# The second mixture of experts as a straight line of tiles, with small tiles between the steps of full ones

## The chip, the cores and the metric

One NeuronCore of a Trainium2 chip runs the whole program. The metric is device time in microseconds of one execution. The kernel before took 1133.65 us, the median of three runs (1132.84 to 1135.4).

## What is computed

Three layers follow one another: an attention with pooled queries, a dense two-layer block (the first mixture), and the second mixture of experts, the only part that the change touches. Its reference, cut to what matters:

```python
def _moe2_ref(x, w_skip, w_gate, w1, w2):          # x 2304 x 512, 8 experts, 512 -> 1024 -> 512
    do_compute = x @ w_skip > 0
    out = x.copy()
    xc = x[do_compute]
    logits = xc @ w_gate
    e_idx = np.argmax(logits, axis=1)
    ...
    for e in range(E):
        mask = e_idx == e
        if not mask.any():
            continue
        h = np.maximum(xc[mask] @ w1[e], 0.0)
        y[mask] = gate_w[mask, None] * (h @ w2[e])
    out[do_compute] = xc + y
```

How many rows an expert gets is known only while the kernel runs.

## The kernel before

Attention and the dense block fill the first 950 us or so. While they run, `Router` places every row in a list in device memory, by expert, and counts. `Router.order` (L525 to L540) sorts the experts by their number of rows. From there on the program speaks of slots k = 0 to 7, the largest expert first. `o[:,0]` holds a slot's number of tiles of 128 rows, `o[:,1]` whether its last tile has at most 32 rows, `o[:,4]` the expert's number.

`Experts.run` (L694 to L778) is the second mixture. Two tiles, "a" and "b", of the expert that is largest so far are begun before the last rows are counted; the slots hold the rest. One full tile is:

- `gather` (L624): an indirect DMA, issued by GpSimd (POOL), brings 128 rows of x into SBUF;
- `turn` (L626): four PE transposes, and a copy out of PSUM on ScalarE (ACT) or VectorE (DVE);
- `layer1` (L635): the product with w1 into two PSUM tiles `ph`, with a relu on ACT (`hh`) and its remainder on DVE (`hl`);
- `layer2` (L650): 24 matmuls of 512 columns with w2 split into a high part `w2hi` and a low part `w2lo`, then `res` on DVE and `put` (L648), an indirect DMA on POOL that scatters the rows into the output.

`split` (L617) makes w2hi on ACT and w2lo on DVE, once for each expert that has full tiles. `few` (L663) handles a tile of at most 32 rows without the split: the product `ph`, a relu `hs`, two transposes, a copy `hT`, the product `py`, four small `res` and a `put`. Its steps wait for each other (PE, ACT, PE, ACT, PE, DVE), and `few` puts the `turn` of two later tiles between them.

`load` (L612) fetches the 4 MB of one expert's w1 and w2 in four DMAs from SyncE's queue (SP). There are three places for weights, a ring W[k%3]; `behind` (L609) lets a POOL memset take the waits for a place's memory.

What sets the order of the work is a tree of branches (L722 to L778). Every engine loads the counts into registers (`values`, L541), and for each slot it asks: is there a load for slot k+2 (L738, SP), has the slot rows (L739), has its last tile at most 32 (L746), is there another tile j (L755 with L757; L755 is the line that the profile names), more than the table ST has (L768), are there gathers for the next slot (L732, POOL). Each engine runs its own copy of the branches. An engine's instructions are issued in the order in which they are written.

```python
for k in range(E):
    if k+2<E:
        with tc.If(ns[k+2]>0): s.load(k+2,ee[k+2])
    with tc.If(n[k]>0) as some:
        with tc.If(few[k]>0) as one:
            s.few(k,xf(k),s.lf[k][:,0],gf(k),f"{k}e",turns(nc.vector))
        with one.Else():
            ...
        with ExitStack() as st:
            for j in range(s.ST[k]):
                st.enter_context(tc.If(n[k]>j+1))
```

With the inputs that are timed, PE executes in this order the tiles a, b, 0f and 0_0 (slot 0), 1e, 1_0 and 1_1 (slot 1), 2f (slot 2), 3e, 4e and 5e (slots 3 to 5); a name with e is a `few` tile, the others are full. Slots 6 and 7 have no rows.

Of the kernel before, what the change touches and what calls it, by code (L numbers as in the profile page):

```python
# [397 lines left out]
class Router:  # L398

    def __init__(s,tc,cp,ident,w9,w9t,NT,E,dram):  # L400
# [7 lines left out]
        s.r7=cp.tile([1,E],F32,name="r7");  # L408
# [4 lines left out]
    def setup(s):  # L413
# [9 lines left out]
        G.tensor_scalar(out=s.far,in0=s.pid,scalar1=float(2*P*s.COLS),scalar2=None,op0=ALU.add)  # L423
        G.memset(s.onesb,1.0)
# [139 lines left out]
    def rest(s,psL):  # L564
# [8 lines left out]
        V.tensor_tensor(out=o[:,3],in0=o[:,3],in1=o[:,2],op=ALU.add)  # L573
        s.o=o
        return [s.values(o[:,i],m) for i,m in ((2,(E-1)*s.TPE+2),(3,E*s.TPE-1),(4,E-1))]

class Experts:

    def __init__(s,tc,router,w1,w2,x2d,out,xT,cp,hp,rp):
        nc=tc.nc; s.tc,s.nc,s.r,s.out,s.x2d,s.hp,s.rp=tc,nc,router,out,x2d,hp,rp  # L580

        s.ST=(4,4,3,3,2,2,2,1)
# [7 lines left out]
    def alloc(s,ctx,psT,psL):  # L590
        tc,E=s.tc,s.r.E
        s.xp=ctx.enter_context(tc.tile_pool(name="exp",bufs=2))
        for k in ("f0","f1","n0","n1"): s.xt[k]=s.xp.tile([P,4,P],F32,name="xt"+k,bufs=1)
# [3 lines left out]
        for k in [f"f{k}" for k in range(E)]+["g0","g1","m0","m1","n0"]: s.xg[k]=one.tile([P,512],F32,name="xg"+k)  # L597
        s.lt=[one.tile([P,s.r.TPE,3],I32,name=f"lt{k}") for k in range(E)]
        s.lf=[one.tile([P,1,3],I32,name=f"lf{k}") for k in range(E)]
# [7 lines left out]
        s.xg["n1"]=s.xg["a"]  # L607
        s.own={"f0":(psL,"lg"),"f1":(s.psY,"py"),"e":(psT,"xt")}
    def behind(s,k):  # L609

        s.nc.gpsimd.memset(s.W[k%3][0][0][:1,0,:1],0.0)
    def load(s,k,e):  # L612
        for t,v in zip(s.W[k%3],(s.w1v,s.w2v)):
            for h in range(2):
                src=v[ds(e,1)][0]
                s.nc.sync.dma_start(t[h],src[:,:,h*512:h*512+512] if v is s.w1v else src[:,4*h:4*h+4])
    def split(s,k,part=("hi","lo"),hs=(0,1),e=None):  # L617

        nc=s.nc
        for h in hs:  # L620
            r,hi,lo=s.W[k%3][1][h],s.hi[h],s.lo[h]
# [10 lines left out]
    def psum1(s,own,nm):  # L632
        p,t=s.own.get(own,(s.psH,"ph"))
        return p.tile([P,4,P],F32,tag=t,name="ph"+nm)
    def layer1(s,k,x,nm,hs,own=None):  # L635
        nc=s.nc; w1=s.W[k%3][0]
        hh=s.hp.tile([P,2,4,P],F32R,tag="xh",name="hh"+nm); hl=s.hp.tile([P,2,4,P],F32R,tag="xl",name="hl"+nm)
        for h in range(2):
            ph=s.psum1(f"{own}{h}",f"{nm}_{h}")
# [10 lines left out]
    def layer2(s,k,lt,g,nm,hs,j=0,own=None):  # L650
# [9 lines left out]
        res=s.res[2 if own else j%2]  # L660
        nc.vector.scalar_tensor_tensor(out=res,in0=py,scalar=lt[:,1:2].bitcast(F32),in1=s.xg[g],op0=ALU.mult,op1=ALU.add)
        s.put(res,lt)
    def few(s,k,x,lt,g,nm,between):  # L663

        nc=s.nc; n=s.r.FEW; w1,w2=s.W[k%3]; cols=lambda j: slice(j*n,(j+1)*n)
        both=s.psum1("e",nm).rearrange("p f c -> p (f c)"); ph,ht=both[:,:256],both[:,256:].rearrange("p (f c) -> p f c",f=2)
# [8 lines left out]
        for _ in between: pass  # L675
# [18 lines left out]
    def run(s,steps,psL):  # L694
# [3 lines left out]
        with ExitStack() as c:  # L698
# [20 lines left out]
            for k in range(2,E): lists(k)  # L719
# [137 lines left out]
```

## Time and profile before

| what | us |
|---|---|
| median of three runs | 1133.65 |
| the profiled execution, its own time | 1134.37 |
| its span, first to last instruction | 1132.6 |
| PE busy (share of the span) | 1060.0 (94%) |
| DVE, ACT, POOL busy | 749.6, 590.0, 347.4 |

The profile was taken of one execution. Its time of 1134.37 us is the span and 1.77 us around it; it lies 0.72 us above the median. The profile names engines PE (TensorE), PEld (its weight loads), DVE, ACT, POOL and SP; a letter q behind a name is that engine's sequencer, where branches, register loads and semaphores run, which do not count as busy. PEclk is the granted TensorE clock as a share of 2.4 GHz; 0.50 is 1.2 GHz. A bracket behind a row of the timeline is the idle time just before it and what ended that.

### The profile page before, as it was taken

The page shows a single profiled execution, that of the slowest core. Times are in us where ns is not written, and L with a number is a line of the kernel's source. Part 1 is how long each engine was busy: PE and PEld are TensorE (multiplying, and loading weights), DVE is VectorE, ACT ScalarE, POOL GpSimd, SP SyncE. Part 2 cuts the span into 40 slices and gives each one's busy share as a digit, 9 for nine tenths or more (in the row PEclk, how much of TensorE's full clock was granted, in tenths as well). Part 3 has the DMA queues.
Part 4 walks back from the last instruction along what each step waited for, and adds up shares of the span by engine and source line. Part 5 has one row for each costly group of instructions (what it writes and reads, how often), then busy time and mean ns, then how long its engine had stood idle before and what let it go on. Part 6 is the DMA issues. An engine that isn't in the chain of part 4 may idle for free. (4 is left out here: it accounts for less than half of the span.)

```text
span 1132.6 us, 20661 instructions
## 1 busy us (share of the span) xinstructions
PE 1060.0 (94%) x7463; PEld 862.6 (76%) x7463; DVE 749.6 (66%) x1870; ACT 590.0 (52%) x1366; POOL 347.4 (31%) x505
## 2 busy tenths in 40 slices
PE   7999999999999999999889999999999999998952
PEld 6677777777677777776679999999999988887831
DVE  6788777887788777875777467777776754313220
ACT  5788778887788787875443333333233324112200
POOL 4466554555666544540430000000000002241000
PEclk8999999999999999999999999999999999998986
DMA  8776646656775556521541101101011015584440
GB/s 215 173 182 183 171 131 160 170 161 172 181 181 168 141 156 154 152 70 47 164 129 64 38 20 38 38 2 38 1 38 39 1 39 205 177 275 166 171 162 8
DMA packets 67661, 135.25 MB, mean 119 GB/s; under 512 B 10684, under 2 KB 19900, under 8 KB 67520
## 3 DMA queue, kind: packets, MB, share of 16 engines
q1 hardware_dynamic: 65056, 127.64, 39.4%
q0 software_dynamic: 2464, 5.80, 1.8%
q8 instruction: 80, 1.31, 0.5%
q14 instruction: 61, 0.50, 0.1%
HBM read 94.63 MB, written 20.17 MB: 101 GB/s over the span
## 5 line engine op out<-in xcount | busy, mean ns | idle before, releaser
L163 PE MATMUL t<-ident,p 128*128 128x128 f32 x1152 | 197.8, 281 | 8.4 <-ACT PT L168 7.8
L163 PEld LDWEIGHTS t<-ident,p 128*128 128x128 f32 x1152 | 137.7, 141 | 70.4 <-ACT PT L168 27.4
L168 ACT ACTIVATE PT<-t 128x384 f32<-128x384 f32 x288 | 140.3, 492 | 61.5 <-PE t L163 57.6
L348 PE MATMUL ph<-xh,wih 128*128 128x256 f32 x576 | 162.3, 282 | 9.4 <-DVE e L354 8.5
L178 PE MATMUL o<-PT,v 128*64 128x256 f32 (+1 forms) x1152 | 170.3, 418 | 0.0
L348 PE MATMUL ph<-xh,wil 128*128 128x256 f32 x576 | 160.7, 279 | 0.2 <-DVE wil L329 0.2
L348 PE MATMUL ph<-xl,wih 128*128 128x256 f32 x576 | 160.6, 279 | 0.0
L113 PE MATMUL s<-ks,qh 128*128 128x384 f32 x384 | 131.6, 397 | 4.6 <-ACT qh L65 2.6
L120 DVE TENSOR_REDUCE m<-s 128x1 f32<-128x768 f32 x128 | 122.4, 956 | 16.4 <-PE s L113 5.2
L356 ACT ACTIVATE gh<-e 128x256 fp32r<-128x256 f32 x144 | 60.3, 419 | 139.2 <-DVE e L354 139.2
L83 POOL TENSOR_TENSOR kl<-kr,kh 64x288 fp32r<-64x288 f32 x120 | 97.0, 839 | 94.8 <-ACT kh L79 87.8
L348 PEld LDWEIGHTS ph<-xh,wih 128*128 128x128 f32 x576 | 108.1, 188 | 21.0 <-issue 14.2
L352 ACT ACTIVATE e<-ph 128x256 f32<-128x256 f32 x144 | 54.9, 382 | 126.3 <-PE ph L348 125.9
L522 POOL DMA_INDIRECT rowlist<-meta,sl x18 | 18.3, 1019 | 333.2 <-DVE sl L521 330.4
L136 ACT ACTIVATE p<-s,nb 128x768 f32<-128x768 f32 x128 | 115.2, 900 | 0.0
L366 PE MATMUL px<-woh,gh 128*128 128x512 f32 x288 | 114.6, 398 | 0.0
L366 PE MATMUL px<-wol,gh 128*128 128x512 f32 x288 | 113.7, 395 | 0.0
L353 DVE TENSOR_SCALAR e<-e 128x256 f32<-128x256 f32 x144 | 56.4, 392 | 86.4 <-ACT e L352 85.1
L348 PEld LDWEIGHTS ph<-xl,wih 128*128 128x128 f32 x576 | 108.4, 188 | 5.0
L366 PE MATMUL px<-woh,gl 128*128 128x512 f32 x288 | 112.1, 389 | 0.0
L167 DVE COPY PT<-t 128x384 f32<-128x384 f32 x144 | 79.5, 552 | 48.9 <-PE t L163 47.5
L113 PE MATMUL s<-ks,ql 128*128 128x384 f32 x384 | 111.2, 344 | 0.0
(304 smaller groups left out, 2021.1 us busy)
## 6 DMA issues: line engine op xcount, KB each, us to landing
qr<-qT SPq DMA_DIRECT2D x64, 288.0 KB, 8.5
w<-w SPq DMA_DIRECT2D x16, 1024.0 KB, 11.6
v<-vt SPq DMA_DIRECT2D x32, 288.0 KB, 3.1
kr<-kT SPq DMA_DIRECT2D x15, 576.0 KB, 6.2
ks<-kh SPq DMA_DIRECT2D x30, 288.0 KB, 4.0
ks<-kl SPq DMA_DIRECT2D x30, 288.0 KB, 3.3
d<-w_in SPq DMA_DIRECT2D x16, 512.0 KB, 8.9
d<-w_out SPq DMA_DIRECT2D x16, 512.0 KB, 3.8
```

The costliest lines, as they stand in the source:

```text
L83: for c in range(0,S,S//4): e.tensor_tensor(out=st["kl"][o,c:c+S//4],in0=st["kr"][r,c:c+S//4],in1=st["kh"][r,c:c+S//4].bitcast(F32),op=ALU ...
L113: nc.tensor.matmul(dst[:,ci,:S3],st[n][j][:,t*P:t*P+P],st["ks"][j][:,c*S3:c*S3+S3],start=first,stop=last)
L120: nc.vector.tensor_reduce(out=m2[:,0:1],in_=s2[:,:,:S3],op=ALU.max,axis=AX.XY)
L136: nc.scalar.activation(pt[:,:2*S3].rearrange("p (c s) -> p c s",c=2),d["s2"][:,:,:S3],AF.Exp,bias=d["nb"],scale=SC,accum_out=a2[:,n,0:1])
L163: nc.tensor.transpose(po[:,c],pt[:,(g*3+c)*P:(g*3+c+1)*P],ident)
L167: if evac[g]: nc.vector.tensor_copy(o,s)
L168: else: nc.scalar.activation(o,s,AF.Copy)
L178: nc.tensor.matmul(cell["o"][64*a:64*a+64,:n],state[pr]["v"][a][:,c],src[:,c,a,:n],start=(c==0),stop=(c==NC-1))
L348: nc.tensor.matmul(ph[:,:TB],w[:,cc],x[:,cc],start=(n==0),stop=(n==3*KC-1)); n+=1
L353: nc.vector.tensor_scalar(out=e,in0=e,scalar1=1.0,scalar2=-1.0,op0=ALU.min,op1=ALU.add)
L356: nc.scalar.activation(gh,e,AF.Copy)
L366: nc.tensor.matmul(X[b][t][:,:DM],a[:,t*P:(t+1)*P],w,start=(f==0 and i==0),stop=(f==KF-1 and i==2))
```

## The change

Two tables of constants take the place of the tree. `TILES=(2,2,1,0,0,0,0,0)` says how many full tiles each slot gets and `SMALL=(0,1,0,1,1,1,0,0)` whether it gets a small one. The tiles are written as one line of code, and the small ones are cut into their steps (`few` is now a generator): few(3) runs between the steps of tile (1,0), and few(1,2) and few(4) alternate. What the tables don't cover is counted into `s.more`; behind one branch at the end there are loops over the remaining tiles for all eight slots.

```diff
+        s.TILES=(2,2,1,0,0,0,0,0); s.SMALL=(0,1,0,1,1,1,0,0)
...
+        for e in range(E): G.memset(s.tiles[:,e:e+1],float(s.TILES[e])); G.memset(s.small[:,e:e+1],float(s.SMALL[e]))
...
-        V.tensor_tensor(out=o[:,3],in0=o[:,3],in1=o[:,2],op=ALU.add)
+        V.tensor_tensor(out=fw,in0=o[:,1],in1=s.small,op=ALU.mult)
+        V.tensor_tensor(out=o[:,1],in0=o[:,0],in1=fw,op=ALU.subtract)
+        V.tensor_tensor(out=o[:,1],in0=o[:,1],in1=s.tiles,op=ALU.subtract)
+        V.tensor_scalar(out=o[:,1],in0=o[:,1],scalar1=0.0,scalar2=None,op0=ALU.max)
+        with s.nc.allow_low_precision(reason="whole numbers"): V.tensor_reduce(out=s.more,in_=o[:,1],op=ALU.add,axis=AX.X)
...
-        s.ST=(4,4,3,3,2,2,2,1)
+        s.ring=(0,1,2,2,0,1,0,0); s.TILES,s.SMALL=router.TILES,router.SMALL
...
-        hs=s.hp.tile([P,2,4,P],F32R,tag="xh",name="hs"+nm).bitcast(F32).rearrange("p a b c -> p a (b c)")[:,0,:256]
+        hs=s.xp.tile([P,256],F32,tag="fs",name="hs"+nm)
         nc.scalar.activation(hs,ph,AF.Relu)
-        next(between)
+        yield
...
-            lists(0); lists(1)
-            first(0); more(0,0); first(1)
+            for k in (0,1,3): lists(k)
+            for k,j in ((0,0),(0,1),(3,0),(1,0)): bring(k,j)
             for _ in l1: pass
             s.split(0,"lo",(1,))
-            s.behind(1); s.load(1,ee[1])
-            for k in range(2,E): lists(k)
+            s.behind(1)
+            for k in (2,4,5): lists(k)
+            s.load(1,ee[1]); s.load(3,ee[3])
+            for k,j in ((1,1),(1,2),(4,0),(2,0),(5,0)): bring(k,j)
...
+            tile(0,0,last=lambda: turn(0,1))
+            tile(0,1,last=lambda: (turn(3,0),turn(1,0,nc.vector)))
+            s.load(4,ee[4])
+            s.split(1)
+            few(3,0,0)
+            tile(1,0,{1:[go(3)],6:[go(3)]},lambda: turn(1,1))
+            s.load(2,ee[2])
+            tile(1,1,last=lambda: (turn(1,2),turn(4,0,nc.vector)))
+            s.split(2)
+            few(1,2,1)
+            few(4,0,0)
+            turn(2,0); turn(5,0,nc.vector)
+            go(1)(); go(4)(); go(1)()
+            s.load(5,ee[5])
+            go(4)()
+            tile(2,0)
+            few(5,0,1)
+            go(5)(); go(5)()
+
+            with tc.If(r.values(r.more,E*r.TPE,None)[0]>0):
+                n=r.values(r.o[:,0],r.TPE,None); left=r.values(r.o[:,1],r.TPE,None)
+                for k in range(E):
+                    with tc.If(left[k]>0):
+                        s.ringd=s.ring; s.ring=(0,)*E
+                        s.load(k,ee[k])
+                        s.split(k)
+                        with tc.For_i(s.TILES[k],n[k],1) as j:
...
```

In the new code `tile(k,j,during,last)` is layer1, then `last()`, then layer2; `during` maps a step of layer1 (eight steps, 0 to 7) to what runs behind it, and `go(k)` runs the next step of few(k). The table `ring` says which of the three places of weights a slot uses.

Two places of the new order are shown, on PE and on SP. First PE, from the end of slot 3 to the end of tile 4e in the kernel before (`ph4e`, `py4e`: the two products of the small tile; `pt`: a turn):

```order
L755 UNCONDITIONAL_BRANCH x3
L739 UNCONDITIONAL_BRANCH
L738 UNCONDITIONAL_BRANCH
L739 COMPARE_AND_BRANCH
L732 UNCONDITIONAL_BRANCH x2
L746 COMPARE_AND_BRANCH
L668 MATMUL ph4e<-w_1_0_11918,xtf_11877 32x256 x2
L629 MATMUL pt5f<-ident,xgf_11893 128x128 x4
L672 MATMUL ph4e<-ident,hs4e 128x128 x2
L629 MATMUL pt_0_14573<-ident,xgg_11896 128x128 x4
L678 MATMUL py4e<-w_1_0_11920,hT4e 32x128 x16
L746 UNCONDITIONAL_BRANCH
```

Three tests (L739, L732 on POOL only, L746) and the jumps to them stand ahead of the tile, and one jump behind it.

The same tile on PE in the changed kernel, with its neighbours (`pf` is the small tile's first product; the row before is the end of tile (1,1), the last one the start of tile (2,0)):

```order
L664 MATMUL py_1_12620<-w2lo_11905,hh_1_12568 128x512 x4
L675 MATMUL pf1e<-w_1_0_11924,xt_11896 32x256 x2
L675 MATMUL pf4e<-xT,xt_11897 32x256 x16
L637 MATMUL pt_0_12691<-ident,xg_11919 128x128 x4
L637 MATMUL pt_0_12697<-ident,xg_11922 128x128 x4
L679 MATMUL pf1e<-ident,hs1e 128x128 x2
L679 MATMUL pf4e<-ident,hs4e 128x128 x2
L685 MATMUL py1e<-w_1_0_11926,hT1e 32x128 x16
L685 MATMUL py4e<-xT,hT4e 32x128 x32
L647 MATMUL ph_0_0_12797<-xt_11898,w_2_0_11928 128x128 x16
```

No branch stands between the tiles any more, and the first step of the second small tile and two turns stand where the first one waits for ACT. (Rows that repeat a step with another half of the weights are left out.)

Second SP's queue, in the kernel before, around the loads of slots 2 and 3:

```order
L738 COMPARE_AND_BRANCH
L616 DMA w_2_1_11925<-w 128x4x512
L738 UNCONDITIONAL_BRANCH x2
L739 COMPARE_AND_BRANCH
L746 COMPARE_AND_BRANCH
L755 COMPARE_AND_BRANCH x2
L732 UNCONDITIONAL_BRANCH
L768 COMPARE_AND_BRANCH
L738 COMPARE_AND_BRANCH
L616 DMA xT<-w 128x4x512
```

SP walks through the same tests as the computing engines before it comes to the next slot's load.

And in the changed kernel, the last list and the first and last piece of some loads (w_1 is place 1, w_2 place 2, xT place 0):

```order
L715 DMA lt_11911<-rowlist 128x9
L624 DMA w_1_0_11924<-w 128x4x512
L624 DMA w_1_1_11927<-w 128x4x512
L624 DMA w_2_0_11928<-w 128x4x512
L624 DMA xT<-w 128x4x512
L624 DMA w_2_1_11931<-w 128x4x512
L624 DMA w_1_0_11924<-w 128x4x512
L546 TENSOR_LOAD more
L768 COMPARE_AND_BRANCH
```

All lists now come ahead of the first load; the loads of slots 1 and 3 follow each other at once, then those of slots 4, 2 and 5, each held only by the readers of its place.

## Rows read from the trace of the kernel before

**Rows 1.** The page's first line: the span.

```profile
span 1132.6 us, 20661 instructions
```

**Rows 2.** Windows: busy us (instructions) of PE, PEld, DVE, ACT, POOL; PEclk, DMA share, GB/s.

```profile
980.00:990.00 10.00, 10.00 (x67) 8.97 (x66) 1.38 (x2) 1.69 (x3) 0.00 (x0) 1.00 1.01 372
...
1080.00:1090.00 10.00, 3.48 (x78) 2.74 (x74) 2.76 (x6) 0.77 (x2) 0.88 (x1) 0.92 1.03 358
1090.00:1100.00 10.00, 7.42 (x70) 4.79 (x74) 1.32 (x2) 0.77 (x2) 0.00 (x0) 0.56 0.20 75
```

**Rows 3.** Timeline of PE's weight loads, one full tile: start, us, what.

```profile
990.01 7.34 PEld L642 LDWEIGHTS ph0f<-xtf,xT 128*128 128x128 f32 x64
...
997.27 0.47 PEld L629 LDWEIGHTS pt1f<-ident,xgf 128*128 128x128 f32 x4
...
997.71 0.47 PEld L629 LDWEIGHTS pt<-ident,xgg 128*128 128x128 f32 x4
...
1003.63 7.34 PEld L642 LDWEIGHTS ph<-xtn,xT 128*128 128x128 f32 x64
```

**Rows 4.** Timeline of PE: tile b, small tiles, and gaps ahead of them.

```profile
976.95 7.22 PEld L642 LDWEIGHTS phb<-xtf,xT 128*128 128x128 f32 x64 [0.68 <-issue]
...
1019.95 3.42 PE L668 MATMUL ph1e<-w,xtf 128*32 128x256 f32 x32 [2.75 <-PEq L755]
...
1031.50 8.82 PE L642 MATMUL ph<-xtn,w 128*128 128x128 f32 x52 [3.11 <-issue]
...
1062.22 7.73 PE L642 MATMUL ph2f<-xtf,w 128*128 128x128 f32 x64 [2.69 <-ACT w2hi L622]
...
1078.13 1.93 PE L668 MATMUL ph3e<-xT,xtf 128*32 128x256 f32 x32 [1.71 <-PEq L755]
...
1081.61 1.96 PE L678 MATMUL py3e<-xT,hT3e 128*32 128x128 f32 x64
1091.25 1.03 PE L668 MATMUL ph4e<-w,xtf 128*32 128x256 f32 x2 [7.69 <-PEq L755]
...
1107.35 1.89 PE L668 MATMUL ph5e<-w,xtf 128*32 128x256 f32 x10 [6.11 <-PEq L755]
...
1114.03 1.96 PE L678 MATMUL py5e<-w,hT5e 128*32 128x128 f32 x64
```

**Rows 5.** Sequencer rows of L755 and L739: count: min/median/max ns, first and last start.

```profile
L755 PEldq COMPARE_BRANCH  x15: 65/191/7222, 999.7 to 1121.8; - x15
...
L739 PEldq COMPARE_BRANCH  x3: 85/4386/4769, 1106.7 to 1126.7; - x3
```

**Rows 6.** Register loads on PE (L543), the same columns.

```profile
L543 PEldq TENSOR_LOAD <-ro x2: 595/598/602, 975.4 to 976.1; - x2
```

**Rows 7.** Timeline of the end: the last result, its scatter.

```profile
1116.05 1.47 DVE L680 SCALAR_TENSOR_TENSOR res<-py5e,lf,xgf 32x128 f32<-32x128 f32 x4 [1.27 <-PE py5e L678]
1117.80 0.87 POOL L649 DMA_INDIRECT out<-res,lf  x1 [13.87 <-DVEq L755]
```

**Rows 8.** The closing line L853 and the scatters of L649, by source.

```profile
L853 POOLq DRAIN  x3: 46/107/3670, 1122.5 to 1132.3; - x3
...
DMA to landing us min/median/max: 2.9/6.2/8.7
```

**Rows 9.** SP's timeline, SP's waits (us in total, times, longest), and weight loads' landing.

```profile
977.82 2.78 SPq L616 DMA_DIRECT2D w<-w  x4
...
SPq L616 <- PEq L755: 46.8, 3, 31.2
...
w<-w SPq DMA_DIRECT2D x16, 1024.0 KB, 11.6
```

**Rows 10.** Timeline of ACT: one split's high halves.

```profile
1026.17 3.71 ACT L622 ACTIVATE w2hi<-w 128x2048 fp32r<-128x2048 f32 x2 [1.33 <-PE py1e L678]
```

**Rows 11.** Timeline of POOL near the start: a memset of the setup, what follows.

```profile
18.85 0.09 POOL L422 MEMSET base<- 128x2 f32 x1
...
25.98 3.07 POOL L83 TENSOR_TENSOR kl<-kr,kh 64x288 fp32r<-64x288 f32 x4 [4.98 <-ACT kh L79]
```

More of the change, by code (lines that the diff above doesn't have):

```diff
@@ L592, in alloc @@
         s.xp=ctx.enter_context(tc.tile_pool(name="exp",bufs=2))
-        for k in ("f0","f1","n0","n1"): s.xt[k]=s.xp.tile([P,4,P],F32,name="xt"+k,bufs=1)
+        for k in range(4): s.xt[k]=s.xp.tile([P,4,P],F32,name=f"xt{k}",bufs=1)
         one=ctx.enter_context(tc.tile_pool(name="ex1",bufs=1))
@@ L596, in alloc @@
         s.hi,s.lo=wt("w2hi",F32R),wt("w2lo",F32R)
-        for k in [f"f{k}" for k in range(E)]+["g0","g1","m0","m1","n0"]: s.xg[k]=one.tile([P,512],F32,name="xg"+k)
-        s.lt=[one.tile([P,s.r.TPE,3],I32,name=f"lt{k}") for k in range(E)]
-        s.lf=[one.tile([P,1,3],I32,name=f"lf{k}") for k in range(E)]
+        s.lt=[one.tile([P,3,3],I32,name=f"lt{k}") for k in range(6)]
+        for k in ["b","d"]+[(k,j) for k in range(6) for j in range(s.TILES[k]+s.SMALL[k])]: s.xg[k]=one.tile([P,512],F32,name="xg%s%s"%(k if type(k) is tuple else (k,"")))
         s.ltd=one.tile([P,1,3],I32,name="ltd")
@@ L716, in run @@
+            bring=lambda k,j: s.gather(s.lt[k][:,j],(k,j))
+            for k in (0,1,3): lists(k)
+            for k,j in ((0,0),(0,1),(3,0),(1,0)): bring(k,j)
             for _ in l1: pass
             s.split(0,"lo",(1,))
-            s.behind(1); s.load(1,ee[1])
-            for k in range(2,E): lists(k)
-            s.turn("n0","f1","b")
-            s.layer2(0,s.lta[:,0],"a","a",hs)
-            two=r.values(r.twof,1,None)[0]
-            n=r.values(r.o[:,0],r.TPE,None); few=r.values(r.o[:,1],1,None); fs=r.values(r.o[:,1],1,[mybir.EngineType.Activation,mybir.EngineType.DVE]); ns=r.values(r.o[:,0],r.TPE); ng=r.values(r.o[:,0],r.TPE,mybir.EngineType.Pool)
@@ new lines, in run, with turn @@
+            s.behind(1)
+            for k in (2,4,5): lists(k)
+            s.load(1,ee[1]); s.load(3,ee[3])
+            for k,j in ((1,1),(1,2),(4,0),(2,0),(5,0)): bring(k,j)
+            xs=[]
+            def turn(k,j,e=None):
+                x=len(xs)%4; xs.append((k,j)); s.turn((k,j),x,f"{k}_{j}",e=e); s.at[k,j]=x
+            s.at={}
+            s.turn("b",3,"b")
+            s.layer2(0,s.lta[:,0],"a","a",ha,0)
+            hb=[]
+            for _ in s.layer1(0,3,"b",hb): pass
+            turn(0,0)
@@ new lines, in run, with tile, few @@
+            s.layer2(0,s.lta[:,1],"b","b",hb,1)
+            i=2
+            def tile(k,j,during={},last=lambda: None):
+                nonlocal i
+                hs=[]
+                for n,_ in enumerate(s.layer1(k,s.at[k,j],f"{k}_{j}",hs)):
+                    for f in during.get(n,()): f()
+                last()
+                s.layer2(k,s.lt[k][:,j],(k,j),f"{k}_{j}",hs,i); i+=1
+            fews={}
+            def few(k,j,n):
+                fews[k]=s.few(k,s.at[k,j],s.lt[k][:,j],(k,j),f"{k}e",n)
+                next(fews[k])
@@ new lines, in run @@
+            go(1)(); go(4)(); go(1)()
[12 more added lines that the diff above has]
+                        with tc.For_i(s.TILES[k],n[k],1) as j:
+                            nm=f"{k}_d"
+                            nc.sync.dma_start(s.ltd,s.lv[:,ds(j+cc[k],1)])
+                            s.gather(s.ltd[:,0],"d")
+                            s.turn("d",0,nm)
+                            hs=[]
+                            for _ in s.layer1(k,0,nm,hs): pass
+                            s.layer2(k,s.ltd[:,0],"d",nm,hs)
+                        s.ring=s.ringd
```

115 lines of the change are left out of this document (29 added, 86 removed).

## The prediction

> **What bounds the kernel now.** I read the page first, then the windows of the last 200 us, the timeline of PE there, the sequencers' rows, and last SP and POOL. The order of instructions on every engine is the same in both kernels up to the second mixture, apart from the setup, so only the stretch from about 976 us to the end of the span [rows 1] is in question.
>
> PE bounds this stretch, but not by its work alone. In straight code it is busy for all of a window, even with the DMA engines full (10.00 of 10 us at a DMA share of 1.01 [rows 2]). Among the small tiles it is busy for 3.48 and 7.42 us of 10, and in the second of these windows the granted clock is 0.56 of 2.4 GHz, so partly 1.2 GHz, after an idle time of 7.69 us [rows 2, 4]. The reader is to see what ends the gaps: four of them, 2.75, 1.71, 7.69 and 6.11 us, end with PE's own sequencer at a branch [rows 4]. A branch of line L755 on that sequencer takes 0.19 us in the median and up to 7.22, one of L739 up to 4.77 [rows 5]: a cheap kind that goes on, and a dear kind that jumps. Behind such a jump there are also gaps with no releaser, 3.11 us in the middle of tile 1_0 [rows 4], which I read as code that has not arrived.
>
> After the last small tile (its matmuls end at 1114.03 + 1.96 = 1115.99 [rows 4]) the span runs for another 16.6 us [rows 1]. PE spends most of them on jumps: two of 4.39 and 4.77 us over the empty slots 6 and 7, the last from 1126.7 to 1131.5 [rows 5], 1.1 us before the end.
>
> **The prices.** A full tile takes 1003.63 - 990.01 = 13.62 us with two turns of 997.71 - 997.27 = 0.44 us each [rows 3], so 12.74 us without. A small tile's matmuls at full clock: 1.93 us for the first product, 1.96 for the second [rows 4], and 0.22 for two transposes (half a turn): 4.1 us. From start to end, waits included, it takes 1081.61 + 1.96 - 1078.13 = 5.4 us [rows 4], so 1.3 us of waiting when nothing fills it.
>
> **The change, part by part.**
>
> *Ahead of tile b.* PE's three register loads go; b begins at 976.95 after 0.68 us of idle time [rows 4], of which the loads are of 0.60 us each, partly hidden [rows 6]. b then begins at 976.3. The four more small DVE operations in the count and the fourth gather on POOL delay only the first load, which has tens of us. The 16 new memsets at 0.09 us at most are 1.4 us of POOL, and an idle time of 4.98 us follows the setup there [rows 11]: nothing. Without that cover they would cost 1.4 us.
>
> *The line on PE from b to the end of few(5).* Six full tiles (b, 0_0, 0_1, 1_0, 1_1, 2_0) are 6 x 12.74 = 76.4 us; nine turns are 4.0; four small tiles 16.3; the last of them has nothing between its steps, 1.3. Three terms the trace doesn't show:
> - Waits in the interleaved small tiles. Their relu stands behind the split's high halves on ACT, 3.71 us for both [rows 10], and 1.9 to 4.7 us of PE work cover that. Bounds 0 and 3.7; I take 1.0, near the lower, since the first half of a split may begin before layer2 has ended.
> - Late code in the straight line. Lower bound 0, by the full window at 980 us [rows 2]; upper 3.11 at each of the four small tiles [rows 4], which run through their code fastest, 12.4. I take 1.5, near the lower bound, as no jump empties what is fetched ahead.
> - The clock. With no gap of over 2 us left I take full clock throughout: 0.
>
> The sum is 976.3 + 76.4 + 4.0 + 16.3 + 1.3 + 1.0 + 1.5 = 1076.8 us for the end of PE's work, where it is 1115.99 now. The Trainium skill ("Runtime: NRT & Kernel Launch", section on instruction fetch mechanics) says that a sequencer fetches the next page of code while it executes the current one and that this is hidden; by that alone the term of 1.5 us would be 0 and the forecast 1086.0. The gap of 3.11 us stands against taking it at its word behind a jump; no row here shows it in a straight line.
>
> *The end.* On PE one register load (0.60 [rows 6]) and one jump over the loops (4.8 as for an empty slot [rows 5]) follow, then 1.1 us: 6.5 us. On POOL the last scatter is issued 1117.80 - 1115.99 = 1.8 us after PE's end [rows 7] and lands 2.9 to 8.7, in the median 6.2 us later [rows 8]; with a register load and the closing 1.1 us that is 9.7 us. Now POOL's drain ends at 1122.5 + 3.67 = 1126.2 [rows 8], 8.4 us after the issue, which would give 11.3. I take 9.7: what is late next at the end is the scatter and no longer PE. Bounds 6.5 and 11.3.
>
> The span is then 1086.5 us. The profiled execution takes 1134.37 us with its span of 1132.6, so 1088.3 against that; it lies 0.72 over the median of 1133.65, which gives **1087.5 us** for a run.
>
> *The loads.* They are moved on SP. Now SP waits for PE's branches, 46.8 us in three times [rows 9]. In the new order they are held by the readers of their place alone. A megabyte DMA lands 11.6 us after its issue in the median [rows 9], about the time of a whole load of four of them at 358 to 372 GB/s [rows 2]. The load of slot 1 is issued at 977.82 now [rows 9] and about 1 us later with one more gather ahead; with that of slot 3 behind it both are there by 979 + 2 x 11.6 = 1002. By the prices above few(3) begins at about 1016. The load of slot 4 follows the first layer of 0_1 (1010), that of slot 2 few(3) (1028 for its second half), needed at 1048. The tightest is slot 5's: its second half waits for few(1,2), at about 1056, and lands by 1062 to 1068; few(5) begins at about 1070. So I cost all of them at nothing, with a cover of 2 us at the worst place.
>
> **The rivals.**
>
> *Late code remains a price of the small tiles.* Instead of 1.5, all four pay 3.11 us: 1087.5 - 1.5 + 12.4 = 1098.4. For it: the gap in tile 1_0 came while the DMA engines were full, and loads run beside three of the four small tiles in the new order too. Against: straight code at 980 us ran without a gap under the same load. Chance 0.14.
>
> *The branches are not what the gaps are made of.* Then the same tiles wait for something else, and the four gaps return: 2.75 + 1.71 + 7.69 + 6.11 = 18.3, so at least 1105.8. The Trainium skill ("Advanced Engine Details and Errata", section on control flow timing) puts a compare-and-branch at about 108 ns; by that figure the 15 of L755 would be an estimate of 1.6 us in all. The rows go against it: up to 7.22 us for one [rows 5], and the matmul ahead of which it stands starts right after. Chance 0.06.
>
> *A load is late.* If the load of slot 5 lands a whole load's time later, few(5) waits up to 11.6 us: 1099.1. For it: the smallest cover; against: nothing else is in the queue then. Chance 0.07.
>
> *The loops behind the branch are entered*, and the kernel gets slower. This is the case in which the change doesn't do what it says: the tables don't cover the rows. Each slot entered pays a load that begins only there (11.6), a split (3.7 and more), and a tile (13.2), nothing of it overlapped: 28.5 us. One slot gives 1116, two 1144.5; from two on it is slower than before. Against: the tiles that ran (two in slot 0 behind a and b, two and a small one in slot 1, one in slot 2, a small one in 3, 4, 5) are exactly the tables. Chance 0.03, two thirds of it for two slots or more.
>
> **The numbers.** My forecast, 1087.5 with 1081.5 to 1094 for its own bounds, has a chance of 0.70. The range reaches up to the rivals of late code and of a late load, 1081 to 1100, which together hold about 0.9 before what I may have missed. A measurement of this kernel can tell about 0.2% (2.3 us) from no change. Faster by more than that are all cases but the entered loops: 0.97; within it 0.01; slower 0.02.
>
> **What would show it.** Right: on PE no idle time above about 1 us between 976 and the end of few(5), with PEclk 1.00; the last small tile's matmuls end near 1077; no L739 or L755 rows, one taken branch on PE of 4 to 5 us; POOL's scatter lands last. Late code would show as idle PE with no releaser among the 32-row matmuls. A late load would show as PE or ACT waiting for a DMA of w. Gaps of the old sizes at the small tiles with another releaser would make my reading of the branches wrong. The prediction is wrong if the end of few(5) lies outside 1074 to 1090, or if the part behind it is still over 13 us.

## The result and the profile after

| | median, us | lowest to highest | runs |
|---|---|---|---|
| kernel before | 1133.24 | 1131.88 to 1135.4 | 4 |
| changed kernel | 1089.81 | 1088.64 to 1090.87 | 4 |

The ratio is 0.9615, with a 95% interval of 0.9596 to 0.9633: 43.4 us faster, against a forecast of 1087.5 in 1081 to 1100. The profiled execution took 1090.87 us with a span of 1089.1.

The first rows of the page of the changed kernel: span [rows 1 before], busy time, granted clock in tenths for 40 slices.

```profile
span 1089.1 us, 20231 instructions
...
PE 1047.0 (96%) x7435; PEld 856.5 (79%) x7435; DVE 745.4 (68%) x1869; ACT 589.3 (54%) x1364; POOL 345.2 (32%) x516
...
PEclk8999999999999999999999999999999999999998
```

The windows of the stretch, with the columns of [rows 2]:

```profile
980.00:990.00 10.00, 10.00 (x78) 9.45 (x78) 1.83 (x3) 1.68 (x3) 7.33 (x9) 1.00 0.87 280
1050.00:1060.00 10.00, 9.74 (x210) 7.29 (x209) 7.24 (x9) 2.94 (x6) 2.76 (x1) 1.00 0.62 214
1070.00:1080.00 10.00, 7.00 (x110) 4.70 (x108) 2.13 (x5) 0.77 (x2) 1.06 (x2) 1.00 0.06 20
1080.00:1090.00 10.00, 0.00 (x0) 0.00 (x0) 0.00 (x0) 0.00 (x0) 0.79 (x1) 0.57 0.03 7
```

The windows of 3.48 and 7.42 us of work at a clock of 0.92 and 0.56 [rows 2] are gone: PE works 9.74 to 10 us of 10 at full clock from tile b until few(5). In the last window PE does nothing, and the span still runs on. PE's timeline, to be held against [rows 4] (matmuls, with the idle time ahead of a row where there is any):

```profile
979.50 7.31 PE L647 MATMUL phb<-xt,xT 128*128 128x128 f32 x64
...
992.68 7.31 PE L647 MATMUL ph<-xt,xT 128*128 128x128 f32 x64
...
1019.57 1.93 PE L675 MATMUL pf3e<-w,xt 128*32 128x256 f32 x32
...
1056.12 1.95 PE L685 MATMUL py1e<-w,hT1e 128*32 128x128 f32 x64 [0.26 <-ACT hT1e L681]
1057.89 1.93 PE L685 MATMUL py4e<-xT,hT4e 128*32 128x128 f32 x64
1059.76 7.41 PE L647 MATMUL ph<-xt,w 128*128 128x128 f32 x64
...
1072.68 1.93 PE L675 MATMUL pf5e<-w,xt 128*32 128x256 f32 x32
1075.18 0.44 PE L679 MATMUL pf5e<-ident,hs5e 128*128 128x128 f32 x2 [0.56 <-ACT hs5e L677]
1076.15 1.95 PE L685 MATMUL py5e<-w,hT5e 128*32 128x128 f32 x64 [0.53 <-ACT hT5e L681]
```

Where four gaps of 1.71 to 7.69 us ended at PE's own branches [rows 4], three of 0.26 to 0.56 are left, all ended by ACT, as a data dependence does. A full tile with one turn takes 992.68 - 979.50 = 13.18 us. The small tiles' rows stand close together, their waits filled by each other's steps.

PE's work now ends at 1078.10, and the span 11.0 us later (16.6 before). The rows of that end, POOL's last scatter and then the sequencers' rows, as in [rows 5, 6, 8]:

```profile
1079.92 0.87 POOL L654 DMA_INDIRECT out<-res,lt  x1 [5.12 <-DVE res L687]
```

```profile
L546 POOLq TENSOR_LOAD <-more x1: 501/501/501, 1080.1 to 1080.1; - x1
...
L768 PEldq COMPARE_BRANCH  x1: 3488/3488/3488, 1078.4 to 1078.4; - x1
L768 POOLq COMPARE_BRANCH  x1: 57/57/57, 1080.7 to 1080.7; - x1
...
L768 POOLq EVENT_SEMAPHORE  x5: 17/42/43, 1083.5 to 1083.8; - x5
...
L768 POOLq INC_SWDGE_SEM  x1: 988/988/988, 1083.9 to 1083.9; - x1
...
L858 POOLq DRAIN  x3: 40/107/3346, 1084.9 to 1088.8; - x3
```

```profile
DMA to landing us min/median/max: 2.1/5.9/9.4
```

The last line is of the scatters of L654; the shortest, 2.1 us, is the last one's. It has landed at 1082.0, and PE's jump is over by 1078.4 + 3.5 = 1081.9. Neither ends last. POOL does: a register load, a branch, 2.8 us of nothing recorded behind it, 1 us of queue bookkeeping, and a drain of 3.35 us, which begins 2.9 us after the landing and is therefore no wait for it.

### The profile page after: what moved, and what is told of

It is laid out like the page before. It is cut to its first block, busy times and chain, and to the rows that moved or that the text cites. A ratio compares the mean times of both kernels' runs of the same rounds, so it can differ in the third digit from the quotient of the medians.

```text
span 1089.1 us, 20231 instructions
## 1 busy us (share of the span) xinstructions
PE 1047.0 (96%) x7435; PEld 856.5 (79%) x7435; DVE 745.4 (68%) x1869; ACT 589.3 (54%) x1364; POOL 345.2 (32%) x516
## 5 line engine op out<-in xcount | busy, mean ns | idle before, releaser
L348 PE MATMUL ph<-xh,wih 128*128 128x256 f32 x576 | 163.5, 284 | 9.2 <-DVE e L354 8.4
L348 PE MATMUL ph<-xl,wih 128*128 128x256 f32 x576 | 162.1, 281 | 0.0
L348 PE MATMUL ph<-xh,wil 128*128 128x256 f32 x576 | 161.1, 280 | 0.2 <-DVE wil L329 0.2
L120 DVE TENSOR_REDUCE m<-s 128x1 f32<-128x768 f32 x128 | 122.4, 956 | 16.6 <-PE s L113 1.2
L348 PEld LDWEIGHTS ph<-xh,wih 128*128 128x128 f32 x576 | 108.2, 188 | 20.9 <-issue 14.1
L178 PEld LDWEIGHTS o<-PT,v 128*64 128x64 f32 x1152 | 70.3, 136 | 53.3 <-issue 22.3
L348 PEld LDWEIGHTS ph<-xl,wih 128*128 128x128 f32 x576 | 108.3, 188 | 5.0
```

Of the source, the lines that this page charges most:

```text
L120: nc.vector.tensor_reduce(out=m2[:,0:1],in_=s2[:,:,:S3],op=ALU.max,axis=AX.XY)
L178: nc.tensor.matmul(cell["o"][64*a:64*a+64,:n],state[pr]["v"][a][:,c],src[:,c,a,:n],start=(c==0),stop=(c==NC-1))
L348: nc.tensor.matmul(ph[:,:TB],w[:,cc],x[:,cc],start=(n==0),stop=(n==3*KC-1)); n+=1
```

## The experiments

The runs came in groups, each on one chip: a0_changed, b0_before, e1_serial and e5_shift on chip 3, the e2 to e4 runs on chip 6, e6_five to e9_early on chip 8; the chip of the result above isn't recorded. The kernel before took 1130.67 to 1138.89 us in them, so times compare within a group; each group's kernel before is in the table. The landmarks are read from PE's timeline of each run's profile: the **dense** block from its first to its last matmul of L348, out of xh and wih; **b to 0_0**, from the first matmul of tile b to that of the next tile; **0_1 to end**, from the first matmul of tile (0,1) to PE's last; and the **tail** behind that.

| run | before, us | median, us | ratio (95%) | dense | b to 0_0 | 0_1 to end | tail |
|---|---|---|---|---|---|---|---|
| before, profile shown ahead | | 1133.24 | | 414.58 | | | 16.62 |
| changed, profile shown here | 1133.24 | 1089.81 | 0.9615 (0.9596 to 0.9633) | 417.04 | 13.18 | 72.24 | 10.99 |
| a0_changed | 1138.89 | 1092.05 | 0.9587 (0.9566 to 0.9608) | 416.91 | 16.72 | 72.68 | 10.88 |
| b0_before | 1138.89 | 1137.65 | | 414.53 | | | 16.80 |
| e1_serial | 1138.89 | 1098.27 | 0.9638 (0.9615 to 0.9661) | 416.98 | 20.46 | 77.53 | 11.02 |
| e5_shift | 1138.89 | 1137.76 | 0.9983 (0.9960 to 1.0006) | 414.54 | | | 16.76 |
| e2_skip | 1130.67 | 1091.95 | 0.9654 (0.9638 to 0.9670) | 416.90 | 13.18 | 75.21 | 10.25 |
| e2_through | 1130.67 | 1090.20 | 0.9648 (0.9632 to 0.9664) | 416.88 | 13.18 | 73.05 | 10.20 |
| e3_noloops | 1130.67 | 1083.22 | 0.9578 (0.9562 to 0.9594) | 416.88 | 13.18 | 72.24 | 6.85 |
| e4_sixslots | 1130.67 | 1123.04 | 0.9927 (0.9911 to 0.9944) | 414.56 | | | 7.83 |
| e7_place | 1138.81 | 1091.70 | 0.9591 (0.9570 to 0.9611) | 414.60 | 19.19 | 72.74 | 10.65 |
| e6_five | 1138.81 | 1093.62 | 0.9610 (0.9588 to 0.9632) | 416.97 | 18.21 | 72.05 | 10.37 |
| e8_both | 1138.81 | 1091.01 | 0.9578 (0.9556 to 0.9601) | 414.58 | 17.36 | 72.04 | 9.88 |
| e9_early | 1138.81 | 1089.49 | 0.9565 (0.9543 to 0.9586) | 415.23 | 19.94 | 72.05 | 9.25 |

### a0_changed and b0_before: both kernels again, in another group

No edit.

> The changed kernel once more, beside the others of this call. Question: its first 976 us ran 2.5 us longer than in the profile of the kernel before, as a slow drift of about 0.25 us per 36 us between 600 and 930 us. Theory L (the layout: two small tiles more in the pool cp move every later pool by 64 bytes a partition, and the matmuls of the dense block take longer): the same drift again, b begins at 978 to 980 us. Theory C (the chip or the execution: the two profiles were taken apart): no more drift than in the kernel before run here, b begins within 0.7 us of that one's start less the 0.7 us of register loads.

> The kernel before, unchanged, for its profile on this chip. Theory L: b begins at 976 to 978 us as in its first profile. Theory C: it drifts like the changed kernel here, b begins about 0.7 us after the changed kernel's.

The dense block again takes 2.4 us more in the changed kernel, so this is no accident of one profile, and theory C falls. Tile b's own start decides nothing: it is 976.30 us here and 975.52 in b0_before, both earlier than theory L had them, since the dense block itself begins anywhere from 534.5 to 539.4 us in the profiles. But another thing is new: from b to 0_0 PE loses 3.5 us. PE's timeline and window of a0_changed:

```profile
984.99 0.49 PE L637 MATMUL pt<-ident,xg 128*128 128x128 f32 x3 [0.91 <-issue]
986.42 0.39 PE L664 MATMUL pyb<-w2hi,hhb 128*128 128x512 f32 x1 [0.94 <-issue]
987.13 0.49 PE L664 MATMUL pyb<-w2hi,hlb 128*128 128x512 f32 x1 [0.32 <-issue]
```

```profile
980.00:990.00 10.00, 7.53 (x49) 5.95 (x48) 1.38 (x2) 1.68 (x3) 4.79 (x5) 1.00 0.99 369
```

They are gaps without a releaser in straight code, with the weight loads at a DMA share of 0.99. So straight code is not free of them, as I had taken it to be.

### e1_serial: the small tiles' steps one after the other

```diff
-            tile(1,0,{1:[go(3)],6:[go(3)]},lambda: turn(1,1))
+            go(3)(); go(3)()
+            tile(1,0,{},lambda: turn(1,1))
...
             few(1,2,1)
+            go(1)(); go(1)()
+            s.load(5,ee[5])
             few(4,0,0)
+            go(4)(); go(4)()
             turn(2,0); turn(5,0,nc.vector)
-            go(1)(); go(4)(); go(1)()
-            s.load(5,ee[5])
-            go(4)()
```

> The straight line, but the steps of each small tile stand together, nothing between them; loads and branches as in the changed kernel. Theory A (the gain comes from the branches that are gone; the interleaving hides 1.3 us of waiting at each of three small tiles): 3 to 5 us slower than the changed kernel, 1093 to 1095. Rival (the interleaving carries the gain, as the small tiles are where the kernel before was idle): 15 us or more slower, over 1104.

6.2 us slower than a0_changed in the median. PE's waits:

```profile
PE pyb L664 <- issue: 2.4, 3, 1.0
...
PE pf4e L679 <- ACT hs4e L677: 0.6, 1, 0.6
...
PE py4e L685 <- ACT hT4e L681: 0.5, 1, 0.5
```

Each small tile now has two waits of about half a us, as the rows of pf4e and py4e show. From 0_1 to the end they cost 77.53 - 72.68 = 4.85 us. The other 20.46 - 16.72 = 3.7 us stand ahead of them, in the gaps of tile b that the edit does not touch. So interleaving is worth some 5 us; the branches, and not the waits of the small tiles, were the bulk of the old gaps.

### e2_skip and e2_through: one branch put back, jumped or passed

```diff
+            with tc.If(r.values(r.more,E*r.TPE,None)[0]>0): tile(1,1)
+            i-=1
             tile(2,0)
```

```diff
-            tile(2,0)
+            with tc.If(r.values(r.o[:,0],r.TPE,None)[2]>0): tile(2,0)
```

> The changed kernel with one branch more, ahead of tile (2,0), that every engine jumps: its body is a copy of a full tile, never executed. Theory A (a taken branch costs PE the fetch of the code behind it): PE idles 4 to 8 us ahead of tile (2,0), of which 0.5 is the register load, and the whole is 4 to 9 us slower, with the granted clock possibly at one half behind the gap. Rival (a branch itself costs about 0.1 to 0.2 us; the gaps of the kernel before were other waits): less than 1.5 us slower.

> The changed kernel with tile (2,0) put behind a branch whose condition holds: the branch is passed through, and only the short jump behind the body is taken. Theory A: PE pays a register load of 0.5 to 2 us and a branch of 0.2 us ahead of the tile and a jump of 1 to 2 us behind it, less than half of what the skipped branch costs: 1.5 to 4 us slower. If every branch cost the same, it would be as slow as the skipped one.

In e2_skip a copy of a full tile, never executed, is jumped over. PE's timeline, and the branch on the sequencers of PE and DVE:

```profile
1057.91 1.93 PE L685 MATMUL py4e<-xT,hT4e 128*32 128x128 f32 x64
1061.54 1.91 PE L647 MATMUL ph<-xt,w 128*128 128x128 f32 x15 [1.70 <-DVEq L764]
1064.51 5.63 PE L647 MATMUL ph<-xt,w 128*128 128x128 f32 x49 [1.06 <-issue]
```

```profile
L764 PEldq COMPARE_BRANCH  x1: 241/241/241, 1060.1 to 1060.1; - x1
...
L764 DVEq COMPARE_BRANCH  x1: 76/76/76, 1061.0 to 1061.0; - x1
```

And PE's timeline of e2_through, in which tile (2,0) stands inside a branch that is not taken:

```profile
1059.06 7.40 PE L647 MATMUL ph<-xt,w 128*128 128x128 f32 x64 [0.74 <-issue]
```

PE loses 3.0 us in the first and 0.8 in the second (0_1 to end, against 72.24, which e3_noloops has in the same group), less than the 4 to 8 and the 1.5 to 4 that I expected: a gap ahead of the tile and one without a releaser inside it, the pattern of [rows 4]. Register loads and semaphores come with each branch, so 0.8 is the price of a branch passed with all of them, and 2.2 what the jump adds. The jump itself is 0.24 us on PE's sequencer; here the gap is what PE finds behind it. The two medians differ by 1.75 us, and their ratios can't be told apart. So the direction of my reading holds, and the price does not carry over: a jump over one tile cost less than most of those in the kernel before (up to 7.22 us [rows 5]).

The traces hold a likely reason for the difference. Among the DMA queues they list one, q8, with packets of 16 KB of kind "instruction". PE's branch of 4.64 us in the kernel before, and the queues in that stretch (packets, MB, share; a packet counts whole where it starts, so that a share can pass 100%; 1101.60 to 1106.26 us):

```profile
L755 PEldq COMPARE_BRANCH  x2: 191/2414/4637, 1101.6 to 1106.5; - x2
```

```profile
q8 instruction: 2, 0.03, 4.3%
```

And all that the queues moved around the jump of 0.24 us in e2_skip (1060.10 to 1060.40 us):

```profile
q1 hardware_dynamic: 63, 0.12, 113.0%
```

From 976 us on, eight of PE's branches in the kernel before take over 3 us, 40.4 us in all, some of it beside PE's last matmuls. Each has such packets in it: one in the branch of 3.49 us, two in the others (4.39 to 7.22 us). The jump at the end of the changed kernel, also 3.49 us, has one; the branches of 0.09 to 0.24 us in e2_skip and e2_through have none, and neither have three of 1.1 to 1.8 us in the kernel before. So a dear branch goes together with code being brought. No edit tests this as the cause.

The order of the loads changed along with the branches and was not tested alone. For the largest gap it can be ruled out: the four DMAs of slot 4's weights had landed by 1075.3 us in the kernel before, 16 us ahead of tile 4e.

### e4_sixslots: the kernel before without its two empty slots

```diff
-            for k in range(E):
+            for k in range(6):
```

> The kernel before with six slots instead of eight (slots 6 and 7 have no rows): two taken jumps fewer at the end on PE, 4.39 and 4.77 us in the profile. Theory A: 9.2 us fewer on PE, but POOL's drain then ends last, so 4 to 9 us faster than the kernel before. Rival (the jumps over empty slots run beside something else): under 1.5 us faster.

The slots 6 and 7, which hold no rows, are left out. 7.6 us faster; the tail alone is 8.8 us shorter: the two jumps of 4.39 and 4.77 us on PE [rows 5] did end last in the kernel before.

### e3_noloops: the changed kernel without the branch and the loops behind it

```diff
-            with tc.If(r.values(r.more,E*r.TPE,None)[0]>0):
-                n=r.values(r.o[:,0],r.TPE,None); left=r.values(r.o[:,1],r.TPE,None)
...
```

> The changed kernel without the last branch and the loops behind it (they are not executed with these inputs): the part after few(5) then has no register load, no jump. Theory S (the scatter is late at the end: it lands 2.1 us after its issue, and POOL's drain waits for it): 0 to 1 us faster. Theory J (POOL's own jump and its bookkeeping stand ahead of its drain of 3.3 us: register load 0.5, 2.8 until it goes on, 1.0 for the semaphore): 3 to 5 us faster, the end 6 to 8 us after few(5) instead of 11.0.

This leaves out the loops, which these inputs never enter. The tail falls from 11.0 to 6.85 us. POOL's closing rows in e3_noloops:

```profile
L841 POOLq DRAIN  x3: 40/107/4455, 1078.6 to 1083.6; - x3
```

The drain follows the scatter at once: it ends at 1083.02, 3.35 us behind the scatter's end on POOL (1078.80 + 0.87). So the branch at the end, never taken into the loops, costs about 4.1 us of POOL's way, as theory J expected (against e2_through in the same group 3.4 in the tail and 0.8 on PE; the medians differ by 7.0, of which the rest is not placed by these two profiles: e2_through's is of its fastest execution, e3_noloops' of its slowest).

### e5_shift and e7_place: where the dense block's 2.4 us come from

e5_shift is the kernel before with the changed kernel's two new tiles of the router's first pool (unused), which move all that lies behind by 64 bytes:

```diff
-        s.r7=cp.tile([1,E],F32,name="r7");
+        s.r7=cp.tile([1,E],F32,name="r7"); s.tiles=cp.tile([1,E],F32,name="tiles"); s.small=cp.tile([1,E],F32,name="small")
```

> The kernel before with the two small tiles of the change reserved in the pool cp, and not used: nothing but the addresses of what comes after them moves. Theory L: 2 to 3 us slower than the kernel before, all of it between 600 and 930 us. Theory C: no difference, within 0.2%.

The time did not change: 414.54 us, so theory L in the form that 64 bytes alone cost the time falls; this run fits theory C, but a0_changed does not. In the changed kernel, though, not everything moves alike: tiles and small move the activations (xh) by 64 bytes, while fw and more, which lie in a later pool, move the weights (wih) by 128. e7_place undoes only that:

```diff
-        s.r7=cp.tile([1,E],F32,name="r7"); s.tiles=cp.tile([1,E],F32,name="tiles"); s.small=cp.tile([1,E],F32,name="small")
+        s.r7=cp.tile([1,E],F32,name="r7"); s.tiles=cp.tile([1,E],F32,name="tiles"); s.small=cp.tile([1,E],F32,name="small"); s.fw=cp.tile([1,E],I32,name="fw"); s.more=cp.tile([1,1],I32,name="more")
...
-        t=lambda x: s.sp.tile([1,E],I32,name=x,bufs=1)
-        fw,s.more=t("fw"),s.sp.tile([1,1],I32,name="more",bufs=1)
+        fw=s.fw
```

> The changed kernel, with its two small new tiles (fw and more, 32 bytes a partition each) put into the pool that lies ahead of everything, so that all that lies behind moves by the same 128 bytes against the kernel before; in the changed kernel the activations' pools moved by 64 and the weights behind the router's pool by 128. Not one instruction is added, removed or moved. Theory P (the dense block of the first mixture takes 416.9 us where it took 414.5 because its two operands lie 64 bytes further apart): the time from its first to its last matmul goes back to 414.5 (414.3 to 414.8), the kernel is 2.4 us faster than the changed one, ratio to the kernel before lower by 0.002. Rival Q (it is the number of instructions, the longer setup, or code that lies elsewhere): it stays at 416.9, and the time with it. Between 415.2 and 416.4 neither holds.

The dense block takes 414.60 us again, with the order of instructions untouched: theory P holds. The group of its first product in the kernel before, in the changed kernel and in e7_place (count | busy us, mean ns | idle time ahead and what ended it):

```profile
L348 PE MATMUL ph<-xh,wih 128*128 128x256 f32 x576 | 162.3, 282 | 9.4 <-DVE e L354 8.5 <-ACT wih L328 0.9
```

```profile
L348 PE MATMUL ph<-xh,wih 128*128 128x256 f32 x576 | 163.5, 284 | 9.2 <-DVE e L354 8.4 <-ACT wih L328 0.9
```

```profile
L348 PE MATMUL ph<-xh,wih 128*128 128x256 f32 x576 | 162.3, 282 | 9.3 <-DVE e L354 8.4 <-ACT wih L328 0.9
```

Two ns more for one matmul, 1.2 us in this group of 576; the line's two other groups, out of xl and wih and out of xh and wil, take 1.5 and 0.4 us more (the busy times of groups overlap a little). The idle time is the same. That the distance between the operands is what counts I infer from the two placements without a loss (all moved by 64, all by 128) and the one with it (64 and 128); other distances weren't tried. (e9_early, with the placement of e7_place, has 415.23 us: 0.7 us more of idle time ahead of this group, 10.0 in all, at the same 282 ns.) The run's total gained nothing over a0_changed (0.9591 against 0.9587), because its tile b lost 6.0 us to gaps without a releaser where a0_changed lost 3.5.

### e6_five, e8_both, e9_early: towards a faster version

e6_five puts the last small tile between the steps of the last full one, e8_both adds this to e7_place, and e9_early adds an earlier register load:

```diff
-            tile(2,0)
-            few(5,0,1)
-            go(5)(); go(5)()
+            tile(2,0,{5:[lambda: few(5,0,1)]},lambda: (go(5)(),go(5)()))
```

```diff
+            mv=r.values(r.more,E*r.TPE,None)[0]
             tile(2,0,{5:[lambda: few(5,0,1)]},lambda: (go(5)(),go(5)()))
 
-            with tc.If(r.values(r.more,E*r.TPE,None)[0]>0):
+            with tc.If(mv>0):
```

> The changed kernel with the last small tile, few(5), put between the steps of the full tile (2,0), in place of behind it; the same instructions otherwise. Theory A (what PE does in straight code is its time; the last small tile pays its waits because nothing fills them): the two waits of 0.56 and 0.53 us go, and the result that ends the program is made by one DVE instruction (about 0.75 us) in place of four (1.47): 1.1 + 0.7 = 1.8 us faster than the changed kernel (1.0 to 2.5). Rival R (the load of slot 5 is then late: few(5) begins some 6 to 8 us earlier than 1072.7, where its first weights landed at 1058 to 1061 and its second at 1065 to 1068): PE waits for a DMA in tile (2,0) and the time is the same or up to 5 us longer.

> Both edits: the two small tiles placed ahead of everything, and few(5) between the steps of tile (2,0). If theories P and A hold, their gains add: 2.4 + 1.8 = 4.2 us faster than the changed kernel (3.0 to 5.0). If Q holds, 1.8; if Q and R hold, no gain or a loss.

> As the one with both edits, and the register load of the count of rows left (one on every engine, ahead of the branch over the loops) put ahead of tile (2,0), in place of behind the last tile. Theory J (what ends last is POOL's way behind its last scatter: register load, jump, bookkeeping, drain): the load of 0.5 us goes from the end, which gets 0.5 us shorter (to about 9.8 from PE's last matmul to the end of the span with the shorter result), and PE pays at most 0.6 us in the middle for its own load, or nothing if its sequencer runs ahead: between 0.5 us faster and 0.1 slower than the one with both edits. Rival S (the end is the scatter's landing or the jump alone): the part behind the last matmul stays as it is and the kernel is the same or 0.6 us slower.

e6_five: no wait for a DMA, so rival R falls. But its gain is 0.2 us on PE (72.05 against 72.24) and 0.6 in the tail, not 1.8: I had let the transposes and the second product follow each other, and one wait stays, as PE's timeline of e6_five shows.

```profile
1073.80 1.95 PE L685 MATMUL py5e<-w,hT5e 128*32 128x128 f32 x64 [0.74 <-ACT hT5e L681]
```

The gain is smaller than the spread of the gaps of tile b, and the median of 1093.62 shows none. e8_both: the placement's 2.4 us add to that on the landmarks, and its median is 2.6 us below that of e6_five in the same group; against a0_changed it shows 1.0 us of the 4.2 expected, the rest being lost in tile b. e9_early: the tail is 0.63 us shorter than in e8_both, and PE pays nothing (72.05 against 72.04), as theory J expected. The sequencers' rows of e9_early:

```profile
L546 POOLq TENSOR_LOAD <-more x1: 508/508/508, 1071.3 to 1071.3; - x1
```

```profile
L856 POOLq DRAIN  x3: 40/107/3346, 1086.5 to 1090.4; - x3
```

The drain is again 3.346 us to the ns, so it looks like a fixed piece of work here. e9_early has the lowest ratio of all versions that keep the loops, 0.9565. Its interval overlaps that of a0_changed (0.9566 to 0.9608), so the totals don't settle that it beats the changed kernel; on the landmarks outside tile b it is 1.7 + 0.6 + 1.6 = 3.9 us better than a0_changed. What the landmarks gave was partly lost in tile b, as PE's timeline and windows of e9_early show:

```profile
985.92 1.10 PE L646 MATMUL phb<-xt,xT 128*128 128x128 f32 x4 [1.62 <-issue]
```

```profile
980.00:985.00 5.00, 3.50 (x27) 3.05 (x26) 0.00 (x0) 0.00 (x0) 3.79 (x4) 1.00 0.97 349
985.00:990.00 5.00, 3.04 (x12) 2.57 (x12) 1.18 (x2) 1.46 (x3) 1.00 (x1) 0.51 1.03 388
990.00:995.00 5.00, 5.00 (x19) 4.02 (x18) 0.21 (x1) 0.33 (x1) 0.00 (x0) 0.81 1.04 397
```

The gaps of 0.35 to 1.62 us sum to 3.5, and b to 0_0 is 6.8 us longer than 13.18: the rest is the granted clock, which falls to 0.51 (so partly to 1.2 GHz) once PE's work thins out, and is 0.81 in the window after.

**What stays open** is the cause of these gaps. All six profiles of the changed kernel and its variants in the two groups with a kernel before of 1138.8 or 1138.9 us (chips 3 and 8) have them, and none of the four in the other two groups, so a difference between chips isn't ruled out either. They begin 6.5 to 7.8 us after tile b, so always at about the same place of PE's code, and always within 10 us of the start of the loads of slots 1 and 3. Late code and the loads' start would both give that. Holding the loads back by some 8 us would tell them apart; it wasn't tried. On chip 3 the kernel before has such gaps too, at another place, in tile 0f (b0_before: 0.33 and 0.92 us; e5_shift: 3.4 us in six), some 22 us after its tile b and after the load of slot 1 begin; the profile shown ahead has none there. In e5_shift the next load is issued only at 1004.86 us, when those gaps are nearly over, so there at least no load's start makes them. They are no price of the change alone either way.

Two more things in the traces bear on it. First, ACT is late in the same stretches. ACT's timeline in the shown profile, in a0_changed and in b0_before, the relu of the second half of tile b, b and 0f:

```profile
986.84 0.60 ACT L649 ACTIVATE hhb<-phb 128x512 fp32r<-128x512 f32 x1 [2.98 <-PE phb L647]
```

```profile
988.03 0.60 ACT L649 ACTIVATE hhb<-phb 128x512 fp32r<-128x512 f32 x1 [3.84 <-remote]
```

```profile
1005.81 0.60 ACT L644 ACTIVATE hh0f<-ph0f 128x512 fp32r<-128x512 f32 x1 [12.59 <-remote]
```

In the four profiles of the changed kernel and its variants without gaps this relu begins 0.04 us after the last matmul that it reads. In the six with gaps, the later of tile b's two relus is 4.0 to 8.1 us behind it, in a0_changed both are late (3.6 and 4.1 us, the first due at 980.0, ahead of PE's first gap). In b0_before it is 9.7 us late, and PE waits 5.85 us for it: tile 0f there takes 24.2 us in place of 13.6, so the kernel before loses more in these stretches than a0_changed does. Second, the code packets that fill PE's long branches (see e2_skip) are missing here. All queues of a0_changed from 976 to 996 us:

```profile
q1 hardware_dynamic: 2166, 4.31, 58.5%
q0 software_dynamic: 769, 2.50, 36.3%
q14 instruction: 1, 0.01, 0.1%
```

No packet of q8 moves there, and the one of q14, 8 KB at 984.8 us, comes after both engines have been late. So whatever holds PE up holds ACT up too, and it is not code on its way in the form that the long branches show. The full DMA engines alone are not it either: PE works through 980 to 990 us at a DMA share of 1.01 in the kernel before [rows 2].

## Why the prediction was right

The result lies in the range, 2.3 us over the forecast, and in the main for the reasons given: PE was held up by its branches, and without them it works through. That it came so close is in part luck: the three steps were off by +3.2, -1.9 and +1.3 us, and partly cancel. By the steps of the sum, in the shown profile:

| step | forecast, us | measured, us |
|---|---|---|
| tile b begins | 976.3 | 979.5 |
| b to the end of PE | 100.5 | 98.6 |
| end part | 9.7 | 11.0 |
| span | 1086.5 | 1089.1 |

**Tile b's start** is the step that failed: "The order of instructions on every engine is the same in both kernels up to the second mixture, ... so only the stretch from about 976 us to the end of the span [rows 1] is in question". The order is the same, the time is not. Of the 2.5 us by which b starts later than before, 0.5 are there when the dense block begins, 2.46 are the dense block, and the way from it to b gives back 0.4, near the 0.65 expected. e7_place shows the cause of the 2.46 to be the place of two tiles of 32 bytes. The 0.5 is scatter between executions: in a0_changed the dense block begins 3.1 us earlier, and b at 976.30 in spite of its 416.91.

**b to the end of PE** came out 1.9 us shorter. Six full tiles and the turns are as costed (12.74 + 0.44 = 13.18). The waits in the interleaved small tiles were 0.26 us (1.0 taken), those of the last one 0.56 + 0.53 = 1.1 (1.3 taken), the clock full, and late code 0, its lower bound. (Four small tiles at the prediction's 4.11 us are 16.4, not 16.3.) The ground given for the full clock, that no gap of over 2 us is left, does not hold in general: in e9_early the granted clock fell to 0.51 with no gap over 1.62 us.

**Late code** was the term with the widest bounds, 0 to 12.4 us, and both of its faces were seen: 0 in the profile shown here and in the group of e2_skip, 3.5 in a0_changed and up to 7.3 in its variants, if the gaps of tile b are that. If they are, its place was wrong: I expected it at the small tiles and gave as the reason for little of it that "no jump empties what is fetched ahead"; the gaps came in tile b, a full one, behind no jump. The queues speak against it: no packet of q8 moves in those of a0_changed. The Trainium skill's rule of "Runtime: NRT & Kernel Launch", section on instruction fetch mechanics, that fetching in a straight line is hidden, agrees with PE's 10.00 of 10 us in the first profile; the 7.53 of 10 in a0_changed agrees with it only if those gaps are not late code, which no run settles.

**The end part** is 11.0 us, within its bounds of 6.5 to 11.3, but by the other candidate. I had the scatter land last, 6.2 us after its issue; it landed after 2.1. POOL's way is what is left: 1.3 us longer than my sum, close to the 11.3 that the old drain gave. The jump over the loops took PE 3.5 us where 4.8 were costed.

**The rivals.** That the branches were not what the gaps are made of: the four gaps are gone, and one branch put back brings a gap back at its place, though a smaller one (1.70 us and 1.06 behind it); fallen. The Trainium skill's compare-and-branch figure ("Advanced Engine Details and Errata", control flow timing), 108 ns, is near the 0.09 to 0.24 us of PE's rows in e2_skip and e2_through, and far from the 3.49 us of the jump at the end; what a short branch costs PE stands in the gap behind it, while a long one's own row is most of its gap (7.22 and 7.69 us in the kernel before). A late load: the loads of slots 2 and 5 were issued by 1021.53 + 36.98 = 1058.5, and the median landing of a weight DMA is 9.8 us, so about 1068, where the second product of few(5) begins at 1076.15. SP's timeline, its wait for the reader of the place, and the landing in the changed kernel:

```profile
1021.53 36.98 SPq L624 DMA_DIRECT2D w<-w  x8
```

```profile
SPq L624 <- PE pf1e L675: 21.8, 1, 21.8
```

```profile
w<-w SPq DMA_DIRECT2D x16, 1024.0 KB, 9.8
```

The loops were not entered: one branch, no load behind it.

## What to carry to other kernels

A branch that separates tiles costs PE more than its own 0.1 us: here 0.8 us for one passed, 3.0 for one jumped over a tile, and gaps of up to 7.7 behind the long ones of the kernel before, in which the trace shows packets of code; count those packets before you price a branch. Where the usual shape of the work is known, a straight line with one branch at the end for the rest pays off, and the interleaving that it permits is worth the waits that it fills (here about 5 us). Keep the end in view: the last scatter on POOL and what POOL does behind it set the end of the span, and a branch there costs 3.4 to 4.1 us even if it is never entered; load its register early (0.6 us). And when a change adds a small tile, put it where it moves all operands alike, or look at the mean of the matmuls that it doesn't touch: "same order" is not "same time".

## What the runs showed that was not expected

- In the kernel before, PE's branches of over 3 us have one or two 16 KB packets of code in them, and those under 0.3 us none.
- Two tiles of 32 bytes a partition, put between the operands of matmuls that the change does not touch, cost 2.4 us in 415: 284 ns in place of 282 for a matmul of the largest group.
- The drain at the end took 3.346 us in the changed kernel, in e8_both and in e9_early alike; in the changed kernel it begins after the last scatter has landed, so it isn't a wait for that scatter. In e3_noloops it ends 3.35 us behind the scatter's end on POOL; in the kernel before it took 3.670.
- The last scatter landed in 2.1 us with the DMA engines idle, where the scatters before took 2.9 to 8.7 [rows 8].
- Gaps without a releaser in straight code, 3.5 to 7.3 us in all, appear at one place in all profiles of the changed kernel and its variants in two groups, and in none in two others; ACT is late in the same stretches, and no code packet of q8 moves there. A comparison of versions that differ by 2 us has to be made on landmarks that leave this place out.
